# A Nystrom attention and soft-MoE kernel: batch 0 with pairs of weight blocks, a fixed order on TensorE and ScalarE, and a new schedule

## The chip, the cores and the metric

The kernel runs on one core of a Trainium2 chip. The metric is the device time of one execution in microseconds, from three runs of the kernel before the change. TensorE multiplies matrices into PSUM, ScalarE evaluates activations and copies, VectorE does element-wise work, reductions and 32 x 32 transposes, GpSimd (POOL) some element-wise work, and SyncE (SP) issues all transfers.

## The reference, cut to what matters

Three stages follow one another. Sizes: 8 batches, 8 heads, 576 positions, head size 64, 32 landmarks; d_model 512, d_ff 1536; 8 experts with 4 slots each.

```python
q_lm, k_lm = means of q and k over groups of 18 positions      # 32 landmarks
A, Bm, C = softmax(q k_lm'), softmax(q_lm k_lm'), softmax(q_lm k')
Z = Bm' / (norms); six times: Z = 2 Z - Z Bm Z                 # Newton iteration
x = A Z C v                                                     # attention, per head
x = (silu(x w_gate) * (x w_val)) w_out                          # gated layer
logits = x phi; dispatch = softmax over tokens; combine = softmax over slots
out = combine @ experts(dispatch' @ x)                          # soft mixture of experts
```

The weights w_gate, w_val and w_out come as 64-bit floats (their 32-bit values are wanted), which the kernel converts itself.

## The kernel before, in words

**Loop.** A batch has 12 units (j = 0 to 11), one for each block of 128 of the 1536 hidden columns. The product A Z C v is never formed: E holds the transposed softmax A in a high and a low part, and G, a product of the batch's small matrix WB (Z C v) with weight block j, is formed for each unit (`g_product`, line 741; ScalarE rounds it to GH at line 766, VectorE makes the rest GL at line 780). A unit (`unit`, line 949) multiplies G with E, for each half of 288 positions: six matmuls into pg (the gate), six into pv (the value), each as EH GH + EL GH + EH GL (`mm3`, line 940). ScalarE makes u = silu(pg) (line 963, issued by `in_order` at line 313), VectorE hT = u * pv (line 975). hT then gives the logits (`logits`, line 786, tile l), and VectorE transposes it into HB (`transposes`, line 798).

**Slots.** After each group of six matmuls `unit` calls `slot(i)`, so a batch has 48 slots, and slot 4j+i stands behind group i of unit j. All other work is traced in slots: the table `SCHED` gives for each piece of it the slot. `u0` says for batch 0 in which of the four slots of a unit the next G product, the logits of the unit before, and the transposes are issued; `w` and `o` give first slot and span of the conversion of each block of w_cat (gate and value) and of w_out; `p` the slot in which a converted block of w_out is transposed on TensorE (m_wt, `p_transposes`), and the distances to its product with phi (m_p) and to the last step (m_ps, into P_sb, which the logits of that unit need); `at1` and `am1` the slots of the 34 steps of batch 1's attention (`attention`, line 545) and of the 17 steps of its softmax of A (`a_softmax`, line 700); `loads` the order of the first loads in SP's queue; `lv` the slot in which v of batch 2 is loaded. Steps for slots below 0 run ahead of the loop, some of them within batch 0's own attention (`first_attention`, line 362).

**Conversions** (`conversion`, line 230). A block of w_cat (1024 words per partition) or w_out (512) takes one ScalarE instruction for the top bits (`f32_top`, line 177), then on VectorE, for each 512 words, a shift (line 193) and a scalar_tensor_tensor that ors in the low bits (line 194). With `lw` set, ScalarE makes the low bits of the whole block (line 184) and VectorE has only one scalar_tensor_tensor for each 512 words (line 190). At its end a block starts the load of the next one into the same stage (`loads_after`, line 218); w_out has two stages in turn. Converted w_out blocks are also stored to DRAM for the end of the kernel.

**Order.** A scheduler may reorder the instructions of an engine within their dependencies. `keep_order` (line 74) pins an engine to the order of the program. Before the change it pins TensorE from batch 1 on (line 1138), and nothing else. `in_order` keeps exps and silus of ScalarE in their order, since each of the two needs a table load when it follows the other. From batch 1 on, three half units near the exps use Tanh (line 960) and one more VectorE instruction (line 961) in place of Silu.

**Pairs.** `paired` (line 738) says where two units share one G product of 512 columns instead of two of 256: batches 1 to 6 before the change.

**PSUM.** g, m_a, m_c, m_t, m_v, m_wt, m_p and m_ps rotate through three banks (tag x), pg and pv through two each.

Of the kernel before, what the change touches and what calls it, by code (L numbers as in the profile page):

```python
# [10 lines left out]
AF = mybir.ActivationFunctionType  # L11
# [11 lines left out]
NJ = DFF // 128  # L23
# [2 lines left out]
SEG = S // M  # L26

SCHED = {
# [23 lines left out]
}  # L52


# [1 line left out]
def nystrom_softmoe_kernel(  # L56
# [144 lines left out]
    def load_w(j):  # L201
        g = W_STAGE[j]
        t = (big(g, f"wr{j}") if g[0] == "w" else part(int(g[0]), int(g[1]))).bitcast(U64)
        sp.dma_start(t, w_cat[j])
        raw["w", j] = t
# [84 lines left out]
    S_ = SCHED  # L290
# [40 lines left out]
    def landmark(nm, b, hp, dst):  # L331

        with tc.issue_after(fence["sum"]) if "sum" in fence else nullcontext():
            dve.tensor_reduce(dst[:, hp, :], qk_t[nm, b, hp].rearrange("p (m s) -> p m s", s=SEG),
                              axis=AX.X, op=ALU.add)
# [209 lines left out]
    def attention(b):  # L545
        assert b == 1 or ("q", b - 1) in seq
        ks, qs = landmark_tiles()
        for nm, dst in (("k", ks), ("q", qs)):
            for hp in range(4):
                (landmark_pool if b == 1 and S_["lp"][2 * hp + (nm == "q")] else landmark)(nm, b, hp, dst)  # L550
                if hp == 3 and b > 1:
                    load_four("q" if nm == "k" else "k", b)
                yield
        def score_tiles(name):
            ms = [psp.tile([128, 512], F32, tag="pv" if i == 3 else "x", name=name, bufs=2 if i == 3 else 3)
                  for i in (3, 0, 1, 2)]
            return {(1, 1): ms[0], (0, 0): ms[1], (0, 1): ms[2], (1, 0): ms[3]}
# [22 lines left out]
        for name, product, eviction in (  # L580
                ("m_a", lambda half, ms: scores(ms, ks, "q", b, half, range(4)), a_eviction),
                ("m_c", c_product, c_eviction)):
            if together:
                t = score_tiles(name)
                for half in (1, 0):
                    product(half, [t[half, 0], t[half, 1]])
                for half, r in ((1, 1), (0, 0), (0, 1), (1, 0)):
                    eviction(half, r, t[half, r])
                    yield
            else:  # L590
                for half in range(2):
                    ms = [psp.tile([128, 512], F32, tag="x", name=name, bufs=3) for r in range(2)]
                    product(half, ms)
                    for r in range(2):
                        eviction(half, r, ms[r])
                        yield
        if b == 1:
            e_tiles(b)
        elif b < nb - 1:
            load_four("k", b + 1)  # L600
# [135 lines left out]
    G_t = {}  # L736

    def paired(b, j):
        return 0 < b < nb - 1 and not (b == nb - 2 and j >= NJ - 2)

    def g_product(b, j, n):

# [206 lines left out]
    def unit(b, j, slot):  # L949
# [3 lines left out]
        for half in range(2):  # L953
            pg = psp.tile([128, 512], F32, tag="pg", name="pg", bufs=2)
            mm3(pg, b, j, 0, half)
            u = mp.tile([128, HALF], F32, tag="u", name="u", bufs=2)
            by_tanh = 0 < b < nb - 1 and (j, half) in TANH[b > 1]
            if by_tanh:

                act.activation(u, pg[:, 0:HALF], AF.Tanh, scale=0.5)  # L960
# [18 lines left out]

    WARM = [3, 4, 3, 2, 2]  # L980

    TANH = [{(3, 1), (4, 0), (4, 1)}, {(1, 1), (2, 0), (2, 1)}]
    GROUPS = [2, 2, 4, 8, 8, 8, 4]


# [30 lines left out]
                next(gens[c], None)  # L1016

    first_attention(side)
    load_w(5)
    for f in side_pre:  # L1020
        f()
# [74 lines left out]
            todo[48 * a + r].append(sm)  # L1096
    prev = None
    n_ins = lambda: len(nc.cur_bb.bb.instructions)
    for b in range(nb):
        if b == 1:  # L1100
            middle = n_ins()
        for j in range(NJ):
            p = prev
            def slot(i):
# [24 lines left out]
                if not first:  # L1129
                    for gen in todo[48 * b + n]:  # L1130
                        next(gen, None)
                if n == (46 if b == 0 else 45) and b + 1 < nb:
                    g_unit(b + 1, 0)
                if n == (47 if b == 0 else 46):
                    g_low()

            prev = (b, j, *unit(b, j, slot))
# [209 lines left out]
```

## Time and profile before

| | us |
|---|---|
| median of 3 runs | 661.8 (661.73 to 662.54) |
| the profiled execution | 661.27 |
| its span in the profile | 659.2 |
| ahead of the loop | 0 to 39.4 |
| batch 0 on TensorE | 39.4 to 124.3 |
| batches 1 to 7 | 124.3 to some 577 |
| experts and output | 577 to 659 |

The granted TensorE clock is 1.00 from 40 us of the span up to its last slice. Over the span TensorE is busy for 94%, VectorE 72%, ScalarE 46%, GpSimd 11%. Times in the rows are microseconds from the start of the span, unless a mean is given in nanoseconds. A matmul's end is modelled, so a busy TensorE may still be waiting between two matmuls: starts are what to go by.

### The profile page before, as it was taken

To read this page: it belongs to the slowest core of one execution; us is meant where nothing else is said; L and a number is where in the kernel's file an instruction comes from. 1 tells how busy PE (TensorE), PEld (TensorE's weight loads), DVE (VectorE), ACT (ScalarE), POOL (GpSimd) and SP (SyncE) were. 2 spreads that over 40 slices of the span, in tenths; PEclk is the share of its full clock that TensorE was granted. 3 is DMA by queue.
4 is the path that set the end of the run, shared out by engine and by line. 5 is a ranking of instruction groups with operands and counts; after the bars stand their busy time and mean duration, and the time that the engine had idled before them with its cause. 6 is when DMAs were issued, how large, how long until landed. Compare 5 with 4: busy or idle time off the path is not lost. (4 is left out here: it accounts for less than half of the span.)

```text
span 659.2 us, 18308 instructions
## 1 busy us (share of the span) xinstructions
PE 620.1 (94%) x7591; PEld 464.7 (70%) x7591; DVE 471.8 (72%) x1154; ACT 300.1 (46%) x764; POOL 72.6 (11%) x81
## 2 busy tenths in 40 slices
PE   5699899999999999999999999999999999989991
PEld 2576677777777877777777877787778877743561
DVE  4999989889578687859785978597857555550441
ACT  2566985465338223823382338233822442320441
POOL 0410012013011101210120013001300000010000
PEclk9699999999999999999999999999999999999996
DMA  7889774453022222222222231222130596599999
GB/s 283 280 300 340 297 269 146 123 180 95 2 74 85 76 73 77 85 75 73 91 69 75 73 108 55 73 73 74 24 122 2 146 387 223 205 327 348 348 371 330
DMA packets 63298, 106.47 MB, mean 162 GB/s; under 512 B 4976, under 2 KB 33008, under 8 KB 61680
## 3 DMA queue, kind: packets, MB, share of 16 engines
q1 hardware_dynamic: 63216, 105.32, 47.6%
q8 instruction: 59, 0.97, 0.6%
q14 instruction: 23, 0.19, 0.1%
HBM read 91.24 MB, written 12.58 MB: 158 GB/s over the span
## 5 line engine op out<-in xcount | busy, mean ns | idle before, releaser
L313 ACT ACTIVATE u<-pg 128x288 f32<-128x288 f32 x174 | 71.9, 413 | 161.3 <-PE pg L946 152.7
L975 DVE TENSOR_TENSOR hT<-u,pv 128x288 f32<-128x288 f32 x174 | 78.0, 449 | 44.2 <-PE pv L946 37.9
L946 PE MATMUL pg<-EH,GH 128*128 128x288 f32 x384 | 93.9, 325 | 2.3 <-ACT u L313 1.4
L780 DVE TENSOR_TENSOR GL<-g,GH 128x512 fp32r<-128x512 f32 (+1 forms) x122 | 65.5, 568 | 33.6 <-ACT GH L766 33.6
L946 PE MATMUL pg<-EH,GL 128*128 128x288 f32 x384 | 86.1, 299 | 1.4 <-DVE GL L780 1.0
L946 PE MATMUL pv<-EH,GH 128*128 128x288 f32 x384 | 84.3, 299 | 0.3 <-ACT GH L766 0.3
L946 PE MATMUL pg<-EL,GH 128*128 128x288 f32 x384 | 82.7, 296 | 0.0
L946 PE MATMUL pv<-EL,GH 128*128 128x288 f32 x384 | 82.3, 295 | 0.0
L946 PE MATMUL pv<-EH,GL 128*128 128x288 f32 x384 | 82.1, 294 | 0.0
L766 ACT CAST GH<-g 128x512 fp32r<-128x512 f32 (+1 forms) x122 | 54.2, 496 | 55.1 <-PE g L749 55.0
L946 PEld LDWEIGHTS pg<-EH,GH 128*128 128x128 f32 x384 | 59.6, 189 | 25.2 <-issue 18.0
L800 DVE STREAM_TRANSPOSE HB<-hT 128x576 f32<-128x576 f32 x96 | 74.3, 774 | 1.8
L946 PEld LDWEIGHTS pg<-EH,GL 128*128 128x128 f32 x384 | 62.3, 188 | 5.1 <-DVE GL L780 4.2
L946 PEld LDWEIGHTS pv<-EH,GH 128*128 128x128 f32 x384 | 61.6, 188 | 2.4 <-issue 1.8
L946 PEld LDWEIGHTS pg<-EL,GH 128*128 128x128 f32 x384 | 61.6, 188 | 0.7 <-issue 0.7
L946 PEld LDWEIGHTS pv<-EL,GH 128*128 128x128 f32 x384 | 61.5, 188 | 0.7 <-issue 0.7
L946 PEld LDWEIGHTS pv<-EH,GL 128*128 128x128 f32 x384 | 61.6, 188 | 0.5 <-issue 0.5
L749 PE MATMUL g<-w,WB 64*32 64x512 f32 (+1 forms) x976 | 56.5, 510 | 0.4 <-ACT WB L536 0.4
L795 PE MATMUL l<-hT,P_sb 128*32 128x160 f32 (+1 forms) x768 | 44.7, 298 | 1.5 <-DVE hT L975 1.1
L795 PEld LDWEIGHTS l<-hT,P_sb 128*32 128x32 f32 x768 | 15.1, 108 | 40.4 <-DVE hT L975 15.8
L914 PE MATMUL m_d<-HB,HB 32*32 32x384 f32 x864 | 35.2, 491 | 0.0
L914 PE MATMUL m_d<-HB,DN 32*32 32x384 f32 x288 | 35.1, 491 | 0.0
(248 smaller groups left out, 940.4 us busy)
## 6 DMA issues: line engine op xcount, KB each, us to landing
k<-in_kT_dram SPq DMA_DIRECT2D x52, 288.0 KB, 3.8
ffn<-in_w_dram SPq DMA_DIRECT2D x13, 1024.0 KB, 8.8
ffn<-in_w_dram SPq DMA_DIRECT2D x24, 512.0 KB, 8.8
HB<-in_w_cat_dram SPq DMA_DIRECT2D x8, 1024.0 KB, 8.4
v<-in_v_dram SPq DMA_DIRECT2D x8, 1024.0 KB, 5.9
q<-in_qT_dram SPq DMA_DIRECT2D x28, 288.0 KB, 3.0
HB<-in_w_out_dram SPq DMA_DIRECT2D x12, 512.0 KB, 6.2
wr<-in_w_cat_dram SPq DMA_DIRECT2D x4, 1024.0 KB, 9.1
```

Of the source, the lines that this page charges most:

```text
L313: i = act.activation(*a, **kw)
L749: pe.matmul(gs[r][32 * hp:32 * hp + 32, 0:256 * n].rearrange("p (u f) -> p u f", u=n), WB[b % 2][64 * r:64 * r + 64, hp, :], w[64 * r:64 * ...
L766: act.copy(H_, g)
L780: dve.tensor_tensor(out=GL, in0=g, in1=GH, op=ALU.subtract)
L795: pe.matmul(L[32 * c:32 * c + 32, 0:32 * k], P_sb[:, j, :], main[:, 0:k, c, :], start=j == 0, stop=j == NJ - 1)
L800: dve.transpose(HB[b % 2][:, S * j:S * j + S].rearrange("p (t r) -> p t r", r=32), hT[:, 0:S].rearrange("p (t r) -> p t r", r=32))
L914: pe.matmul(ms[a][32 * g:32 * g + 32, 0:384].rearrange("p (j f) -> p j f", j=NJ), d_of(a, g, k), hb[32 * a:32 * a + 32, :, 4 * k + g, :], ...
L946: pe.matmul(ps[:, 0:HALF], G_t[b, j, q, sel_][h], e[:, q, ts_], start=n == 0, stop=n == 5)
L975: dve.tensor_tensor(out=o, in0=u, in1=pv[:, 0:HALF], op=ALU.mult)
```

## The change

It sets a new schedule, extends the pairs to units 4 to 11 of batch 0, adds a Tanh set for batch 0, puts the q landmarks of batch 1 behind its first scores m_a, issues one Silu on a single element behind batch 0's attention, pins TensorE and ScalarE to the program's order in batch 0 (ScalarE only there), lets ScalarE make the low bits of w blocks 5 and 7 to 11, and moves batch 1's first G product from slot 46 to 45.

```diff
 SCHED = {
-    'w': [[-22, 2], [-12, 2], [0, 3], [1, 3], [6, 3], [10, 3], [14, 3], [18, 3], [20, 4], [28, 4], [24, 4], [33, 4]],
-    'o': [[-6, 1], [3, 2], [5, 3], [9, 3], [13, 3], [17, 3], [21, 3], [25, 3], [29, 3], [33, 3], [37, 3], [41, 3]],
-    'p': [[0, 2, 2], [5, 2, 1], [10, 2, 1], [14, 2, 1], [18, 2, 1], [22, 2, 1], [26, 2, 1], [30, 2, 1], [34, 2, 1], [38, 2, 1], [42, 2, 1], [46, 1, 0]],
-    'loads': ['w1', 'q0', 'o0', 'w0', 'v0', 'o1', 'q1', 'v1', 'w2', 'w4', 'p', 'w3'],
-    'at1': [1, 2, 3, 3, 4, 5, 6, 6, 7, 7, 8, 8, 9, 9, 10, 10, 12, 13, 13, 13, 16, 17, 18, 19, 20, 21, 22, 26, 28, 31, 34, 37, 40, 43],
-    'am1': [20, 21, 22, 22, 24, 24, 26, 27, 28, 30, 32, 34, 36, 37, 39, 41, 42],
+    'w': [[-22, 2], [-12, 2], [1, 4], [5, 4], [7, 5], [9, 4], [13, 4], [16, 4], [20, 4], [24, 4], [28, 4], [32, 4]],
+    'o': [[-6, 1], [0, 3], [2, 4], [6, 4], [10, 4], [14, 4], [18, 4], [22, 4], [26, 4], [30, 4], [34, 4], [38, 4]],
+    'p': [[-1, 2, 2], [3, 2, 2], [7, 2, 2], [11, 2, 2], [15, 2, 2], [19, 2, 2], [23, 2, 2], [27, 2, 2], [31, 2, 2], [35, 2, 2], [39, 2, 2], [43, 2, 2]],
+    'loads': ['w1', 'q0', 'o0', 'w0', 'v0', 'o1', 'q1', 'w2', 'w3', 'w4', 'p', 'v1'],
+    'at1': [0, 0, 1, 2, 3, 4, 7, 8, 8, 9, 9, 10, 11, 12, 15, 16, 16, 18, 18, 19, 20, 21, 23, 23, 23, 24, 27, 29, 31, 33, 35, 37, 39, 43],
+    'am1': [11, 12, 13, 13, 19, 19, 27, 28, 29, 30, 33, 35, 37, 38, 39, 40, 44],
...
-    'u0': [1, 3, 3, 0],
+    'u0': [1, 1, 1, 0],
...
-    'lw': [0, 0, 0, 0, 0, 0, 0, 0, 0, 0, 0, 0],
+    'lw': [0, 0, 0, 0, 0, 1, 0, 1, 1, 1, 1, 1],
...
-    'lv': 26,
+    'lv': 28,
 }
...
     def attention(b):
...
-        for nm, dst in (("k", ks), ("q", qs)):
+        def landmarks(nm, dst):
             for hp in range(4):
-                (landmark_pool if b == 1 and S_["lp"][2 * hp + (nm == "q")] else landmark)(nm, b, hp, dst)
+                landmark(nm, b, hp, dst)
                 if hp == 3 and b > 1:
                     load_four("q" if nm == "k" else "k", b)
                 yield
+
+        yield from landmarks("k", ks)
+        if b > 1:
+            yield from landmarks("q", qs)
...
+                if name == "m_a":
+                    yield from landmarks("q", qs)
...
     def paired(b, j):
-        return 0 < b < nb - 1 and not (b == nb - 2 and j >= NJ - 2)
+        return (b > 0 or j >= 4) and b < nb - 1 and not (b == nb - 2 and j >= NJ - 2)
...
-            by_tanh = 0 < b < nb - 1 and (j, half) in TANH[b > 1]
+            by_tanh = b < nb - 1 and (j, half) in TANH[min(b, 2)]
...
-    TANH = [{(3, 1), (4, 0), (4, 1)}, {(1, 1), (2, 0), (2, 1)}]
+    TANH = [{(4, 1), (5, 0), (5, 1)}, {(3, 1), (4, 0), (4, 1)}, {(1, 1), (2, 0), (2, 1)}]
...
     first_attention(side)
+    in_order("silu", warm, one, AF.Silu)
     load_w(5)
...
+    middle = n_ins()
     for b in range(nb):
         if b == 1:
-            middle = n_ins()
+            keep_order(mybir.EngineType.Activation, middle, n_ins())
...
-                if n == (46 if b == 0 else 45) and b + 1 < nb:
+                if n == 45 and b + 1 < nb:
                     g_unit(b + 1, 0)
-                if n == (47 if b == 0 else 46):
+                if n == 46:
                     g_low()
```

The line `keep_order(mybir.EngineType.PE, middle, n_ins())` behind the loop stays; with `middle` taken ahead of the loop it now covers batch 0 too.

## Rows read from the trace of the kernel before

**Rows 1.** Busy time of each engine in three stretches of batch 0 (start:end, length, engines)

```profile
39.40:72.50 33.10, 30.65 (x355) 21.39 (x356) 30.85 (x69) 24.40 (x54) 2.50 (x2) 1.00 0.89 325
72.50:108.00 35.50, 34.69 (x418) 26.19 (x414) 32.20 (x83) 27.91 (x67) 5.05 (x4) 1.00 0.73 270
108.00:124.30 16.30, 16.30 (x172) 12.41 (x171) 15.60 (x33) 7.68 (x22) 1.34 (x2) 1.00 0.51 154
```

**Rows 2.** Waits of TensorE from 39.4 to 124.3: us in total, times, longest

```profile
PE pg L946 <- ACT u L313: 1.4, 2, 0.9
PE pg L946 <- ACT GH L766: 0.9, 1, 0.9
```

**Rows 3.** TensorE in order of time, batch 0 and batch 1 (start, length, what)

```profile
107.05 0.53 PE L946 MATMUL pv<-EH,GH 128*128 128x288 f32 x2
...
108.04 0.66 PE L749 MATMUL g<-w,WB 64*32 64x256 f32 x16
108.63 0.41 PE L285 MATMUL m_ps<-cst,HB 128*128 128x32 f32 x2
...
111.52 0.47 PE L795 MATMUL l<-hT,P_sb 128*32 128x160 f32 x8
111.91 0.54 PE L946 MATMUL pg<-EH,GH 128*128 128x288 f32 x2
...
122.28 1.09 PE L749 MATMUL g<-w,WB 64*32 64x512 f32 x16
123.30 0.54 PE L946 MATMUL pv<-EH,GH 128*128 128x288 f32 x2
...
124.30 0.47 PE L795 MATMUL l<-hT,P_sb 128*32 128x160 f32 x8
124.55 0.43 PE L279 MATMUL m_p<-HB 128*32 128x128 f32 x8
...
133.83 0.53 PE L946 MATMUL pg<-EH,GH 128*128 128x288 f32 x2
...
137.20 0.47 PE L795 MATMUL l<-hT,P_sb 128*32 128x160 f32 x8
```

**Rows 4.** Groups of ScalarE's instructions, 39.4 to 124.3 (busy us, mean ns of one)

```profile
L313 ACT ACT_TABLE_LOAD x5 | 6.4, 1283 | 0.9 <-DVE stat L609 0.9
L177 ACT ACTIVATE w<-HB 128x1024 f32<-128x1024 f32 x6 | 6.9, 1155 | 0.0
L313 ACT ACTIVATE CE<-CE,stat 128x576 f32<-128x576 f32 (+1 forms) x4 | 2.2, 552 | 0.0
L313 ACT ACTIVATE AN<-AN 128x576 f32<-128x576 f32 x2 | 1.4, 684 | 0.0
```

**Rows 5.** Groups of VectorE's instructions, 39.4 to 124.3

```profile
L780 DVE TENSOR_TENSOR GL<-g,GH 128x256 fp32r<-128x256 f32 x24 | 9.1, 414 | 0.0
L193 DVE TENSOR_SCALAR w<-w 128x512 int32<-128x512 int32 x20 | 7.8, 414 | 0.6 <-ACT w L177 0.3
```

**Rows 6.** VectorE in order of time, around 102, 125 and 147

```profile
102.63 1.65 DVE L193 TENSOR_SCALAR HB<-HB 128x512 int32<-128x512 int32 x1
...
125.03 1.28 DVE L780 TENSOR_TENSOR GL<-g,GH 128x512 fp32r<-128x512 f32 x2
...
147.13 0.44 DVE L961 SCALAR_TENSOR_TENSOR u<-u,pg 128x288 f32<-128x288 f32 x1
```

**Rows 7.** ScalarE in order of time, around 70

```profile
69.63 1.28 ACT L313 ACT_TABLE_LOAD   x1
70.93 0.41 ACT L313 ACTIVATE u<-pg 128x288 f32<-128x288 f32 x1
```

**Rows 8.** Transfers of w_out blocks: count, size, median us from issue to landing

```profile
HB<-in_w_out_dram SPq DMA_DIRECT2D x12, 512.0 KB, 6.2
```

**Rows 9.** SyncE's issues in order of time: the load of v for batch 1

```profile
34.95 0.38 SPq L166 DMA_DIRECT2D v<-in_v_dram  x1
```

**Rows 10.** GpSimd in order of time, around 102

```profile
102.33 1.67 POOL L727 TENSOR_TENSOR EL<-AT,EH 128x576 fp32r<-128x576 f32 x1 [4.94 <-ACT EH L726]
```

## The prediction

> **What bounds the kernel now.** I read the profile in this order: busy time by stretch, TensorE's waits, its instructions in order of time, then the groups and timelines of ScalarE and VectorE, last the transfers. A slot is a quarter of a unit, numbered 0 to 47 in a batch; unit j covers slots 4j to 4j+3.
>
> The change touches batch 0 and what stands ahead of it. On TensorE batch 0 runs from the first G product at 39.4 to the first logits of batch 1 at 124.3, 84.9 us in three stretches (slots to 17, to 37, and the rest) [rows 1]. VectorE is busy for 30.85 + 32.20 + 15.60 = 78.65 us of them, 93%; ScalarE for 24.40 + 27.91 + 7.68 = 59.99, 71%. TensorE itself looks 96% busy, and its recorded waits are few: 1.4 us on u and 0.9 us on GH, both from ScalarE [rows 2]. The reader must not stop there: in batch 0 TensorE's busy time is padded. One group of six matmuls that is followed by another kind of work takes 0.99 us (107.05 to 108.04), while 24 in one stream take 3.37 us, 0.84 for six (133.83 to 137.20) [rows 3]. Each interruption so costs 0.15 us. I counted 42 runs of pg/pv matmuls in TensorE's timeline of batch 0, three or four per unit: logits, m_p, m_ps, m_wt and the attention pieces are scattered. So batch 0 is held by VectorE's load and by interruptions, and the later batches are out of reach of this change.
>
> **TensorE's part.** *Pinned order and new slots.* In the code as changed, slot 4j+1 carries G product, logits and m_p together, slot 4j+3 carries m_ps, m_wt and all of batch 1's attention products (3, 7, 11, 15, 23, 27, 31, 35, 39, 43; the m_n of 29, 33, 37 stand in 4j+1). That is two interruptions per unit, 24 for 42: 18 x 0.15 = -2.7 us. Logits followed by m_p take 0.25 us (124.30 to 124.55) where logits followed by pg take 0.39 (111.52 to 111.91) [rows 3]: 12 x 0.14 = -1.7 us. *Grouping.* A single G product takes 0.59 us (108.04 to 108.63), a double one 1.02 (122.28 to 123.30) [rows 3]; units 4 to 11 become four doubles: 8 x 0.59 - 4 x 1.02 = -0.6 us. With these, 5.0 us, TensorE wants 79.9 us with all its waits, and 77.6 without its 2.3 of waits [rows 2]. The other bound is a count of its pieces at undisturbed durations, which I put near 73 as an estimate: it would also mend the two G products that now alternate with other work.
>
> **ScalarE's part.** Five table loads of 1283 ns lie in the stretch [rows 4]. The new Silu on one element draws one of them to before the loop, behind the Newton iteration, where ScalarE has gaps; units (4,1), (5,0), (5,1) by Tanh, leave, as in the later batches, one load into exp and Tanh and one back to Silu: -3 x 1.28 = -3.85 us. Eight G conversions become four doubles, about -0.5 us. Six conversions of w now take their low half from ScalarE: no row shows this Copy from a quarter-stride source. Its nearest row is the Prelu of the same 1024 elements, 1155 ns [rows 4]; below I allow half of that, above twice; I take 1.1: +6.6 us (3.5 to 13.9). Sum +2.2, to about 62 us of ScalarE in 79: not the bound on average. It is uneven, though: the four exps of C (2.2 us) and the two of A (1.4) [rows 4], which stood at slots 13 and 24, now stand in slots 18 and 19 with a table load in front, and the order is pinned.
>
> **VectorE's part.** The same six conversions lose two shifts each. A shift lasts 414 ns [rows 5] and starts some 0.34 before the next instruction: 12 x 0.34 = -4.1 us. The low word is or-ed in by an instruction of the same kind and size as now. GL of two single blocks is four instructions of 414 ns [rows 5], of a double block two in 1.28 us [rows 6]: about -0.1 per block, -0.5 in all with their overlap. Three Tanh halves each add a scalar_tensor_tensor of 0.44, some 0.37 as it overlaps [rows 6]: +1.1 us. The four q landmarks move behind m_a (slots 8 to 10) and the softmax of A to slots 27 to 44: moved work, the same count, and VectorE has no idle place that would hide it, so it costs nothing only as long as nobody waits for it. Demand: 78.65 - 4.1 - 0.5 + 1.1 = 75.1 us.
>
> **A rule on table loads.** Behind the load at 69.63, which lasts 1.28, the next u starts at 70.93, 0.02 later [rows 7]; so I price a load at 1.28. The Trainium skill (ScalarE: Activation LUTs, What ACT_TABLE_LOAD costs) counts a drain of about 1.38 us on top of each switch, 2.66 in all; the trace shows no such time behind this one. By the page the three loads would give back 8.0 us of ScalarE, an estimate.
>
> **Transfers.** The landing of a w_out block is 6.2 us [rows 8]. From block 2 on, a conversion now begins at slot 4j-6, and the stage it uses is loaded again when it ends, two slots later, for the block eight slots on: six slots or 9.6 us, for an issue of 0.4 and 6.2. Covered by 3 us as long as VectorE's last step is on time. In the queue of SP the load of v for batch 1, which can only go out at 34.95 [rows 9], no longer stands ahead of w2, w3, w4 and phi; these go out while it still waits, and v and w5 follow. v is wanted at slot 27. The stores and reloads of w_out move a slot or three earlier with their conversions and pass no other waiting transfer. Worth: w2 and w3 are there when the loop starts; VectorE, which then had q landmarks to fill with, gains nothing that it isn't charged for above. Ahead of the loop the first m_wt can run before the first G product instead of after it, and the table load leaves the first u's path: 0 to -0.6, I take -0.3.
>
> **The sum.** TensorE wants 73 to 79.9 us, VectorE 75.1. Before, VectorE was busy 93, 91 and 96% in the three stretches [rows 1]; with TensorE as close behind it, I take 95%: 75.1 / 0.95 = 79.1 us for 84.9, -5.8. With -0.3 ahead of the loop it is -6.1. The profiled execution took 661.27 us (span 659.2), 0.5 below the median of 661.8; so 655.2 there, and 655.8 against the median: 656.0, rounded. The share at 91% gives 82.5 (-2.4), at 98% 76.6 (-8.3): 653.5 to 659.5 for this case alone.
>
> **Rivals.** *TensorE's floor* (12%): VectorE's queue fits between, waits go to the level of later batches. 73 + 1.5 = 74.5 us, -10: 651.5. For it: the even spread of the new slots. Against: VectorE at 100%.
>
> *The heap in slots 18 and 19* (22%): table load, six exps, two halves of Tanh, m_wt's and m_p's copies in one fixed queue: 1.3 + 3.6 us ahead of everything else in 3 us of TensorE's time. GH of units 6 and 7 (slot 21), the copies of m_wt and m_p and the u of slot 20 all stand behind it, and the pinned TensorE waits at m_ps. Priced at 3 us on top of the forecast: 659. For it: both waits of TensorE [rows 2] are this very thing, in two smaller doses.
>
> *Vector work arriving late behind a pinned queue* (slower, 12%): the top half of each w_out conversion is an instruction of ScalarE in fixed order; if it waits for its transfer, u and GH wait behind it. It decides once VectorE ends a conversion more than the 3 us of cover late. Then ten blocks each wait about 1 us, of which TensorE, also pinned, pays nearly all, and the forecast's 6 us become +3: 664.8. For it: 93% busy, and a shift that stood beside GpSimd's 1.67 us product [rows 10] took 1.65 us instead of 0.41 [rows 6]; the Trainium skill (GPSIMD Engine Reference, Key points) says that the two share SBUF interfaces, and the trace agrees. Four such products of A are moved into slots 29, 30, 39 and 40, beside conversions of w and w_out: 4 x 1.2 = 5 us at worst for 2 to 3 now. Against: the conversions lose 4.1 us of VectorE.
>
> *It does little* (8%): the program's order may already be what ran, so that pinning changes nothing; then pairing gives 0.6 and the loads are off the path: 661.2. Against it: the scattered order [rows 3].
>
> **How the numbers follow.** The forecast has 46%, the rivals 12, 22, 12 and 8. Faster by over 0.2% (1.3 us, about what a measurement of this kernel tells from no change): 46 + 12 + 21 = 79%; within 0.2%: 9%; slower: 12%. The range 650.5 to 662.5 leaves out the slower case and a little below the floor.
>
> **What would show it.** Right: VectorE over 94% busy in the first 70 us after the first G product, TensorE's timeline with two interruptions per unit, two table loads in batch 0, the first G product of batch 1 near 115 (122.28 less the gain and one slot). Wrong: waits of TensorE on u or GH above 3 us together (the heap); ScalarE waiting on w_out transfers (the slower case); VectorE under 88% with TensorE still waiting, which would mean that order, not load, sets the time.

## The result, and the profile after

The change makes the kernel slower: 666.21 us (median of 6 runs, 664.48 to 667.90) for 661.90 (6 runs on the same chip), a ratio of 1.0063 with a 95% interval of 1.0047 to 1.0079. The forecast was 656.0. The profiled execution after took 664.48 us, the shortest of the six, and its span is 662.7; before, 661.27 and 659.2. What follows explains the 3.5 us between these two executions, not the whole 4.3 between the medians.

First, where the 3.5 us between the two spans lie. The busy time by stretch, cut at the first G product of batch 0, the first of batch 1, the last of batch 7 and the end (start:end, length; PE, PEld, DVE, ACT, POOL busy; granted TensorE clock; DMA share; GB/s), for the kernel before:

```profile
0.00:39.44 39.44, 24.82 (x244) 16.61 (x244) 29.23 (x69) 16.05 (x39) 9.18 (x14) 0.87 0.76 261
39.44:122.28 82.84, 79.62 (x912) 58.97 (x912) 76.59 (x180) 58.48 (x139) 8.89 (x7) 1.00 0.77 274
122.28:569.15 446.87, 444.03 (x5646) 348.78 (x5645) 334.49 (x821) 199.13 (x524) 49.81 (x49) 1.00 0.30 99
569.15:659.20 90.05, 71.63 (x792) 40.34 (x791) 31.48 (x86) 26.40 (x63) 4.70 (x11) 0.94 0.99 327
```

and for the kernel after:

```profile
0.00:39.86 39.86, 24.85 (x248) 16.79 (x249) 28.49 (x67) 16.82 (x40) 9.62 (x14) 0.91 0.92 330
39.86:123.48 83.62, 76.59 (x855) 59.90 (x854) 74.72 (x168) 60.27 (x135) 9.62 (x7) 0.96 0.70 239
123.48:569.06 445.58, 443.49 (x5639) 349.02 (x5635) 332.03 (x818) 198.57 (x523) 49.85 (x49) 1.00 0.30 98
569.06:662.70 93.64, 71.96 (x792) 40.31 (x791) 31.57 (x86) 26.38 (x63) 4.76 (x11) 0.94 0.96 315
```

The lengths differ by +0.4, +0.8, -1.3 and +3.6 us. Batch 0, which the change rewrites, is 0.8 longer where 5.8 less were forecast, although TensorE and VectorE both have less to do in it (76.59 for 79.62, 74.72 for 76.59), and its granted clock is no longer 1.00. The largest loss lies in the last 94 us, whose code the change doesn't touch. Of the 1.3 us gained in batches 1 to 7, 0.9 lie in batch 1, which takes 67.5 for 68.4 from its first G product to that of batch 2.

Inside batch 0 the starts of G products, before and then after, cut out unit 1 and units 6 and 7:

```profile
42.42 0.66 PE L749 MATMUL g<-w,WB 64*32 64x256 f32 x16
49.30 0.66 PE L749 MATMUL g<-w,WB 64*32 64x256 f32 x16
...
78.91 0.66 PE L749 MATMUL g<-w,WB 64*32 64x256 f32 x16
94.45 0.62 PE L749 MATMUL g<-w,WB 64*32 64x256 f32 x2
```

```profile
42.98 0.66 PE L755 MATMUL g<-w,WB 64*32 64x256 f32 x16
52.86 1.11 PE L755 MATMUL g<-w,WB 64*32 64x256 f32 x16
...
98.49 1.09 PE L755 MATMUL g<-w,WB 64*32 64x512 f32 x16
```

A unit is counted here from its G product to the next unit's. Unit 1 takes 9.9 us for 6.9. Units 6 and 7, which share the G product at 78.58 (shown below), take 19.9 for 15.5. The other nine units together take 53.8 for 60.4. So a gain of 6.6 us, more than the 5.8 forecast, did come, in part because work was moved out of these units; two places lost 7.4.

**Batch 0.** TensorE's waits from 39.86 on, to be held against [rows 2] (total, times, longest):

```profile
PE m_a L542 <- ACT P_sb L286: 2.1, 1, 2.1
PE m_ps L285 <- ACT HB L280: 1.7, 1, 1.7
PE m_t L638 <- ACT P_sb L286: 1.6, 1, 1.6
```

All three end at copies on ScalarE. What held the first is in ScalarE's order of time:

```profile
45.46 0.43 ACT L313 ACTIVATE u<-pg 128x288 f32<-128x288 f32 x1
48.60 0.66 ACT L177 ACTIVATE HB<-HB 128x512 f32<-128x512 f32 x1 [2.70 <-DMA HB<-in_w_out_dram]
49.16 0.17 ACT L286 COPY P_sb<-m_ps 128x32 f32<-128x32 f32 x1
49.23 0.59 ACT L271 COPY HB<-m_wt 128x512 f32<-128x512 f32 x1
```

and in TensorE's:

```profile
46.57 0.67 PE L542 MATMUL m_a<-q,ks 64*32 64x288 f32 x2
49.38 0.44 PE L542 MATMUL m_a<-q,ks 64*32 64x288 f32 x3 [2.14 <-ACT P_sb L286]
...
51.29 0.68 PE L952 MATMUL pv<-EH,GH 128*128 128x288 f32 x2
51.77 0.68 PE L952 MATMUL pv<-EL,GH 128*128 128x288 f32 x2
```

The top half of w_out block 2, pinned in ScalarE's queue, waits 2.70 us for its transfer. The copies of m_ps and m_wt stand behind it, the PSUM bank that m_a wants is not free, and TensorE, pinned too, stands for 2.14 us. From about 50.5 pairs of matmuls start 0.48 apart, where 0.27 is the step elsewhere: the granted clock falls to the lower level, 0.50 of full speed (1.2 of 2.4 GHz). The same happens after the stalls in units 6 and 7. Both stretches (the columns as above):

```profile
50.50:53.90 3.40, 3.40 (x28) 2.31 (x26) 1.18 (x3) 0.41 (x1) 0.00 (x0) 0.50 0.94 348
88.00:91.40 3.40, 3.40 (x16) 3.33 (x16) 3.40 (x13) 3.26 (x8) 0.00 (x0) 0.50 0.67 195
```

In both TensorE is busy for all 3.40 us, so busy time doesn't show the loss. In the first it is 1.7 us, half the stretch: unit 1 takes 9.9 us, and 6.0 in a version with neither stall nor half clock there (e2_wout_later below, G products at 45.30 and 51.33); the 3.9 between them are the 2.1 of wait and 1.7. For the second no such price is shown; pairs of executions of the same code (below, at h1_three_again) speak against it.

The transfer is late because of what lies ahead of it in SyncE's queue and on the DMA engines. The queue's issues after, the counterpart of [rows 9]:

```profile
35.24 0.38 SPq L166 DMA_DIRECT2D v<-in_v_dram  x1
35.66 0.52 SPq L167 DMA_DIRECT2D v<-in_v_dram  x1
39.53 0.35 SPq L204 DMA_DIRECT2D wr<-in_w_cat_dram  x1
39.93 0.43 SPq L248 DMA_DIRECT2D wo_dram<-HB  x1
40.40 0.43 SPq L215 DMA_DIRECT2D HB<-in_w_out_dram  x1
```

The block goes out at 40.40, behind v and w_cat block 5. That load (39.53) had held the queue, since it waited for TensorE's m_w, and over the whole flight of the w_out block the DMA engines are full (the last but one column):

```profile
SPq L204 <- PE m_w L535: 3.2, 1, 3.2
```

```profile
40.40:48.60 8.20, 6.24 (x64) 4.46 (x56) 8.00 (x17) 3.94 (x11) 0.00 (x0) 1.00 1.01 326
```

It is used 8.20 us later (48.60), where [rows 8] have 6.2 as the median, and ScalarE stood ready from 45.90, 5.5 us behind the issue.

In units 6 and 7 ScalarE runs from 73.3 to 93 us without a gap. A cut of that run, with the counterpart of TensorE behind it:

```profile
82.30 0.40 ACT L966 ACTIVATE u<-pg 128x288 f32<-128x288 f32 x1
82.59 1.12 ACT L177 ACTIVATE w<-HB 128x1024 f32<-128x1024 f32 x1
83.62 1.06 ACT L772 CAST GH<-g 128x512 fp32r<-128x512 f32 x2
84.56 0.29 ACT L280 COPY HB<-m_p 128x128 f32<-128x128 f32 x1
84.72 1.19 ACT L184 ACTIVATE HB<-HB 128x1024 int32<-128x1024 uint16 x1
```

```profile
78.58 2.26 PE L755 MATMUL g<-w,WB 64*32 64x512 f32 x16
...
84.90 0.41 PE L285 MATMUL m_ps<-cst,HB 128*128 128x32 f32 x2 [1.67 <-ACT HB L280]
...
87.83 0.99 PE L638 MATMUL m_t<-cst,CE 128*128 128x128 f32 x4 [1.61 <-ACT P_sb L286]
```

The copy that m_ps needs (84.56) stands behind a table load, the exps, w8's top and GH. The double G product at 78.58 takes 2.26 where the others take 1.09: it has a stall of 1.2 us inside, which is in no list of waits.

**The tail.** Inside the m_d products of the last batch TensorE pauses and waits for nothing that the profile shows:

```profile
584.61 0.48 PE L920 MATMUL m_d<-HB,DN 32*32 32x384 f32 x1
586.44 0.83 PE L920 MATMUL m_d<-HB,HB 32*32 32x384 f32 x4 [1.35 <-issue]
```

In the third part of the page of the profile a queue of its own carries instructions. Its size fits TensorE's code: 59 packets of 16 KB for 2 x 7527 matmuls and weight loads make 64 bytes for one instruction, 256 for a packet. In the trace a packet of it runs from 584.05 to 585.12, just ahead of the pause; before, packets run at 574.54 and 586.41, on either side of m_d. The pairs of batch 0 take 128 instructions from TensorE (7591 to 7527 of each kind), half a packet. The four weight loads of the experts that m_d's end releases go out from 587.32 on, not 585.27, and the transfers, the bound of the tail, lose a stretch. The same window before and then after:

```profile
585.00:590.00 5.00, 4.26 (x33) 2.14 (x30) 3.97 (x13) 0.32 (x1) 2.98 (x4) 1.00 0.98 318
```

```profile
585.00:590.00 5.00, 3.60 (x27) 1.76 (x22) 2.60 (x6) 0.09 (x1) 2.87 (x4) 1.00 0.60 191
```

### The profile page after: what moved, and what is told of

It is laid out like the page before. It is cut to its first block, busy times and chain, and to the rows that moved or that the text cites. A ratio compares the mean times of both kernels' runs of the same rounds, so it can differ in the third digit from the quotient of the medians.

```text
span 662.7 us, 18185 instructions
## 1 busy us (share of the span) xinstructions
PE 616.9 (93%) x7527; PEld 466.0 (70%) x7527; DVE 466.8 (70%) x1137; ACT 302.0 (46%) x761; POOL 73.8 (11%) x81
## 5 line engine op out<-in xcount | busy, mean ns | idle before, releaser
L981 DVE TENSOR_TENSOR hT<-u,pv 128x288 f32<-128x288 f32 x171 | 76.6, 448 | 44.6 <-PE pv L952 40.3
L952 PE MATMUL pv<-EH,GH 128*128 128x288 f32 x384 | 82.6, 296 | 0.0
L801 PEld LDWEIGHTS l<-hT,P_sb 128*32 128x32 f32 x768 | 15.1, 108 | 44.0 <-DVE hT L981 15.8
```

The lines of the kernel that those rows point to most:

```text
L801: pe.matmul(L[32 * c:32 * c + 32, 0:32 * k], P_sb[:, j, :], main[:, 0:k, c, :], start=j == 0, stop=j == NJ - 1)
L952: pe.matmul(ps[:, 0:HALF], G_t[b, j, q, sel_][h], e[:, q, ts_], start=n == 0, stop=n == 5)
L981: dve.tensor_tensor(out=o, in0=u, in1=pv[:, 0:HALF], op=ALU.mult)
```

## The experiments

Seventeen runs were made, each in five rounds beside the kernel before, on five chips (one for each group of names, e1 to e4, e5 to e8, f, g and h); sixteen kernels, one of them twice (f3 and h1). Median and ratio are over the executions of a run. The rest of the ledger comes from TensorE's instructions in one profiled execution, which lies up to 2.6 us off its median; f3 and h1 agree within 0.3 us in each of the four lengths. The columns: start (to the first G product), batch 0 (to the first of batch 1), batches 1 to 7 (to the last G product), tail (to the end of the span), and where in the tail instruction packets start, counted from that last G product. The first m_d product starts at 10.6 there in all of them; the last column has the start of the last one.

| kernel | median | ratio, 95% | start | batch 0 | 1 to 7 | tail | packets at | last m_d |
|---|---|---|---|---|---|---|---|---|
| before | 661.9 | | 39.4 | 82.8 | 446.9 | 90.0 | 5.4, 17.3 | 15.6 |
| after | 666.2 | 1.0047-1.0079 | 39.9 | 83.6 | 445.6 | 93.6 | 15.0, 18.4 | 17.7 |
| e1_no_pairs | 662.1 | 0.9991-1.0018 | 40.5 | 83.8 | 446.5 | 90.3 | 1.7, 16.8 | 15.6 |
| e2_wout_later | 660.7 | 0.9975-1.0002 | 42.2 | 78.7 | 445.8 | 93.8 | 15.1, 18.7 | 17.9 |
| e3_scalar_free | 661.3 | 0.9969-1.0003 | 41.4 | 81.0 | 446.0 | 91.2 | 15.0 | 15.6 |
| e4_no_low_by_scalar | 663.6 | 1.0014-1.0053 | 41.8 | 80.7 | 447.2 | 94.3 | 15.6, 18.9 | 18.2 |
| e5_later_b6 | 661.8 | 0.9983-1.0013 | 39.5 | 79.5 | 451.3 | 90.9 | 1.7, 16.8 | 15.6 |
| e6_before_b6 | 666.3 | 1.0055-1.0085 | 38.3 | 82.9 | 452.1 | 92.0 | 15.4 | 15.6 |
| e7_after_b6 | 665.3 | 1.0035-1.0066 | 39.7 | 85.7 | 448.9 | 90.8 | 1.6, 17.4 | 15.6 |
| e8_later_b6_low78 | 661.5 | 0.9984-1.0023 | 40.8 | 81.2 | 448.6 | 91.1 | 1.7, 16.9 | 15.6 |
| f1_no_silu | 665.6 | 1.0031-1.0074 | 38.4 | 85.3 | 446.0 | 94.3 | 15.5, 19.0 | 18.3 |
| f2_later_no_pairs | 659.5 | 0.9953-0.9981 | 40.9 | 81.0 | 446.7 | 90.9 | 5.8, 16.6 | 15.6 |
| f3_later_no_pairs_no_silu | 658.8 | 0.9939-0.9965 | 39.1 | 81.1 | 445.9 | 90.9 | 5.5, 17.3 | 15.6 |
| f4_f3_scalar_free | 661.8 | 0.9984-1.0002 | 39.3 | 83.7 | 446.2 | 91.1 | 5.9, 16.9 | 15.6 |
| g1_w_later | 661.3 | 0.9984-1.0011 | 39.9 | 84.8 | 446.3 | 91.2 | 6.1, 17.0 | 15.6 |
| g2_ct_spread | 660.8 | 0.9976-1.0001 | 39.8 | 81.1 | 446.5 | 90.8 | 5.8, 17.5 | 15.6 |
| g3_both | 661.2 | 0.9985-1.0007 | 39.1 | 83.2 | 446.2 | 91.2 | 5.4, 16.9 | 15.6 |
| h1_three_again | 658.9 | 0.9955-0.9979 | 39.0 | 80.8 | 446.0 | 90.9 | 5.9, 16.7 | 15.6 |
| h2_only_o2_later | 658.9 | 0.9956-0.9979 | 39.1 | 80.3 | 445.8 | 90.0 | 3.7, 17.1 | 15.6 |

### The tail: pairs and TensorE's code

```diff
-        return (b > 0 or j >= 4) and b < nb - 1 and ...
+        return 0 < b < nb - 1
```

> The changed kernel with batch 0's G products unpaired again, so that TensorE has its 128 instructions back. Theory (the end of the kernel lost 3.5 us because the fetch of TensorE's next block of code fell into the dense m_d products of the last batch's tail): the pause of 1.8 us inside m_d near 584.6 goes, the span from the last batch's last G product (569.1) to the end goes from 93.6 back to about 90.1 us, batch 0 pays 0.6 to 1.2 us for the unpaired products, and the time is about 662 to 663 where the changed kernel shows 664.5. Rival (the loss at the end comes from something else, such as the order of loads or the run itself): the tail keeps its 93.6 us and the time is 665 to 666.

Measured: 4.1 us less than the change by the medians. The pause is gone, the last m_d product starts at 15.6, the tail is 90.3, and batch 0 is only 0.2 longer. Giving back the instructions far from batch 0 separates the code from what batch 0 does:

```diff
-        return ... and not (b == nb - 2 and j >= NJ - 2)
+        return ... and not (b == nb - 2 and j >= NJ - 10)
```

> The changed kernel with the G products of units 2 to 9 of batch 6 taken apart and nothing else. Theory of the code blocks: no pause in m_d, tail 90 us instead of 93.6, unpaired products 0.6 to 1.0 us, so 663.5 against the changed kernel's median of 666.2; batch 0 as in the changed kernel, with both stalls. Rival: the tail keeps 93.6 us and the time is 666 to 667.

> The kernel before, with the G products of units 2 to 9 of batch 6 taken apart and nothing else: 128 instructions more on TensorE, which by blocks of 256 puts the edge where 128 fewer put it. Theory of the code blocks: a pause of 1 to 2 us inside m_d appears, the tail from the last G product to the end goes from 90.0 to about 93.5 us, the unpaired products cost 0.6 to 1.0, and the time is 665 to 666 where the kernel before takes 661.8. Rival: no pause, 662.5.

Measured: the edit is the same, and it moves the tail in opposite ways. In the changed kernel the pause goes and the tail falls from 93.6 to 90.8; in the kernel before, a pause appears and it grows from 90.0 to 92.0. There the packet starts at 15.4 and the pause lies just behind m_d, in the matmuls on the tile warm. TensorE's waits in the tail of e6_before_b6:

```profile
PE warm L808 <- issue: 1.6, 1, 1.6
```

The mechanism held; two sizes did not. The pause in the kernel before is a wait of 1.6 us, and its tail grows by 2.0, not 3.5. And taking 8 units of batch 6 apart costs 3.3 us, not 0.6 to 1.0: batch 6 takes 67.1 for 63.8 in e5, e7 and e8, by the starts of its first G products. In e6 it takes 68.6, and 3.4 us of that batch ran at half clock. Batch 0 of e7 is also 2.1 longer than that of the changed kernel, with the same code. So the whole time hides what the tail gained: only the ledger tells the two theories apart.

In all rows of the ledger a packet that starts between 15.0 and 15.6 goes with a pause of 1.0 us or more, and where none starts there, there is no such pause. Four of the six pauses lie inside m_d (the changed kernel, e2, e4, f1), with tails of 93.6 to 94.3 us. Two lie behind it, with less or no loss: 92.0 in e6, and in e3 91.2, where the kernels without a pause have 90.0 to 91.2. How the packet stops the engine isn't shown.

### The first stall: w_out's transfer

```diff
-    'o': [[-6, 1], [0, 3], [2, 4], [6, 4], [10, 4], ... [38, 4]],
+    'o': [[-6, 1], [0, 3], [4, 3], [8, 3], [12, 3], ... [40, 3]],
```

> The changed kernel with the w_out conversions of blocks 2 to 11 begun two slots later (one slot ahead of where they began in the kernel before), all else as changed. Theory (a conversion of w_out on the pinned ScalarE waits 2.7 us for its transfer, the copies of the first scores stand behind it, TensorE stands for 2.1 us and then goes 3.4 us at half clock): ScalarE's wait for that transfer at 46 to 48.6 goes, TensorE's wait at m_a and the stretch of half clock near 50.5 to 53.9 go, the first scaled product of batch 1 comes about 3.5 to 4 us sooner, and the time is about 661. Rival (the copies wait for their place in ScalarE's queue anyway, or the time comes back as a wait at a later slot): less than 1 us.

Measured: 5.5 us less by the medians. ScalarE's wait and TensorE's wait at m_a are gone, batch 0 is 4.9 shorter, and up to 55 us its clock stays up:

```profile
39.00:55.00 16.00, 14.76 (x167) 10.97 (x166) 14.89 (x32) 9.39 (x23) 0.00 (x0) 1.00 0.86 298
```

The 3.9 of unit 1 are most of the 4.9. The tail keeps its pause (93.8), as the code theory wants.

With batch 6 taken apart on top of it (the edit of e7_after_b6):

```diff
-        return ... and not (b == nb - 2 and j >= NJ - 2)
+        return ... and not (b == nb - 2 and j >= NJ - 10)
```

> The kernel with the later w_out conversions (660.7 us), and the G products of units 2 to 9 of batch 6 taken apart, which gives TensorE back the 64 weight loads and 64 products that pairing takes away in batch 0, but far from batch 0. Theory (TensorE's code comes in blocks of 256 instructions, and 128 instructions fewer put a block's edge into the dense m_d products of the tail, under a full DMA load): the pause of 1.5 us inside m_d goes, the tail from the last G product to the end goes from 93.8 to about 90.2 us, the unpaired products cost 0.6 to 1.0, and the time is about 658. Rival (the tail's loss has to do with what batch 0 does): the pause stays, and the time is 661 to 662.

Measured: 661.8, a miss in the sum and a hit in its part. The tail is 2.9 shorter, batch 6 takes 3.3 more, and batch 1, which the edit doesn't touch, 2.2 more (69.8 for 67.6): 3.4 us of it, from 144.9, ran at half clock.

### The start: one table load

```diff
-    in_order("silu", warm, one, AF.Silu)
```

> The changed kernel without the one line that loads ScalarE's Silu table ahead of the loop. Theory (that load moves a conversion and the copies of the Newton steps, TensorE's products before the loop come in another order, and TensorE stands for 1.3 to 1.9 us before it at 32 us, after which some executions have a stretch of half clock): that wait is 0.4 us as in the kernel before, the first scaled product starts at 38.5 to 39.5, a table load of 1.3 us falls into the first units instead; time 0.5 to 1.5 us less than the changed kernel's 666.2, so about 665. Rival (the load ahead of the loop costs nothing, and inside the loop it would): 1.3 us more, 667.5.

In the changed kernel the load stands at 25.23, ahead of a conversion of w and of the copies of the Newton steps, and TensorE's instructions of the start come in another order: all of m_v first, then a wait for a copy behind two conversions on VectorE.

```profile
30.32 0.90 PE L419 MATMUL m_v<-v,CT 128*32 128x64 f32 x40
32.77 0.68 PE L469 MATMUL m_n<-newton 128*128 128x128 f32 x4 [1.55 <-DVE newton L503]
```

Without that line, in f1_no_silu:

```profile
29.97 0.65 PE L419 MATMUL m_v<-v,CT 128*32 128x64 f32 x32
31.02 0.49 PE L469 MATMUL m_n<-newton 128*128 128x128 f32 x2 [0.40 <-DVE newton L503]
```

The start is 1.5 shorter (38.4), as expected, and nearly all of it is lost at once: the same w_out block goes out 1.5 sooner (38.89), but is there only 0.5 sooner (48.14). ScalarE now waits 3.8 us for it, TensorE 3.4 at m_a, and batch 0 is 1.7 longer. The time is 0.6 less. Of the nine profiled executions of kernels with this load, five (e2, e3, e4, e8, f2) show a granted clock under 1.00 between 30 and 40 us, and their starts end at 40.8 to 42.2; the other four end at 39.5 to 40.5. Of the ten without it none does, and they end at 38.3 to 39.9. That the changed kernel's other runs, up to 3.4 us above its profiled one, are executions of the first sort fits this but isn't shown.

### ScalarE's pin and its low halves

```diff
-        if b == 1:
-            keep_order(mybir.EngineType.Activation, middle, n_ins())
```

> The changed kernel with ScalarE's order in batch 0 left to the scheduler, TensorE still pinned. Theory (the pin on ScalarE makes both stalls): ScalarE takes the copies of the scores ahead of the late conversion, both stretches of half clock go, and the time is 657 to 660. Rival (the stalls come from where the work was put, not from the pin): ScalarE's order hardly differs, and the time stays at 664 to 666; a third way is that the scheduler puts conversions ahead of what TensorE waits for, and the time is over 667.

```diff
-    'lw': [0, 0, 0, 0, 0, 1, 0, 1, 1, 1, 1, 1],
+    'lw': [0, 0, 0, 0, 0, 0, 0, 0, 0, 0, 0, 0],
```

> The changed kernel with all low parts of the weights converted by VectorE, none by ScalarE (6 instructions of 1.1 to 1.2 us less on ScalarE, about 4.1 us more on VectorE). Theory (ScalarE's heap of work at 73 to 93 us makes the second stall: two low parts, a table load, exponentials and a high part in one run): the heap gets 2.3 us shorter, the second stall of 4.8 us and perhaps its stretch of half clock shrink, and the time is 1 to 3 us less than the changed kernel's. Rival (VectorE is the bound of batch 0, as the prediction had it): batch 0 gets about 4 us longer and the time is 668 or more.

Measured: 4.9 and 2.7 us less by the medians, the first short of its expectation (661.3 for 657 to 660). Without the pin the copies pass the late conversion and m_a no longer waits, but one stretch of half clock stays (3.4 us from 54.2). From the G product of unit 6 to that of unit 8 it takes 15.9 us (79.76 to 95.62), like the kernel before (78.9 to 94.5, 15.6), where the changed kernel takes 19.9. So the pin is part of both stalls; its removal is no gain by itself, though: f4_f3_scalar_free (below) loses by it. Without ScalarE's low halves the second stretch of half clock is gone (1.00 from 73 to 108 us), units 6 and 7 take 16.9, and VectorE's 4.4 us more (80.05 busy for 75.61, from 39 to 125) didn't make batch 0 longer: 80.7. VectorE's load did not set the time.

### Repairs together

The edits of e1 and e2; those and f1's; and those and e3's:

> The changed kernel with w_out conversions two slots later and batch 0's G products unpaired: both repairs found so far together. Theory (they act in different places, transfers in batch 0 and code blocks in the tail): no pause in m_d, tail about 90.2 to 91 us, no stretch of half clock near 50 us, and the time is 660.7 less 3 plus 0.2 to 1, about 658.3. Rival (unpaired products cost in batch 0 what they cost in batch 6, 3.4 to 5 us for 8 units): 661 to 662.

> As the kernel with later w_out conversions and unpaired products, and also without the Silu load ahead of the loop. Theory (three separate losses): the first scaled product starts near 39 in place of 40 to 42, and the time is 1 us less, about 657.5, faster than both kernels. Rival (the table load inside the loop costs what the start gains): the same time.

> As the kernel with all three repairs, and ScalarE's order in batch 0 left to the scheduler. Theory (the pin holds copies that TensorE waits for behind conversions): the wait at m_ps and m_t near 78 to 90 us gets shorter by 1 to 2 us, time about 656.5. Rival (ScalarE is full there whatever the order): 657.5 or more.

Measured: 659.5, 658.8 and 661.8. Later w_out conversions and no pairs take 6.7 us off the changed kernel, leaving out the table load another 0.8; with all three the kernel beats both, though each of the three times lies above its expectation. Freeing ScalarE on top costs 3.0: TensorE then waits 2.3 for bd and 2.6 for low halves. The third kernel run again, the same code on another chip:

> The kernel with all three repairs once more, the same code. If its ratio of 0.9952 was that of the kernel, it comes out at 0.994 to 0.997; if it was that of few runs, at 0.998 to 1.0.

Measured: 658.9, ratio 0.9967 (0.9955 to 0.9979), inside the first expectation: this version beats both kernels.

The two executions of this code also bear on the price of the half clock in units 6 and 7. One stretch in f3 and then in h1:

```profile
80.10:86.90 6.80, 6.59 (x28) 6.00 (x28) 5.93 (x19) 6.48 (x16) 1.71 (x2) 0.50 0.81 266
```

```profile
80.10:86.90 6.80, 5.84 (x66) 4.75 (x67) 5.91 (x19) 6.71 (x16) 1.96 (x2) 1.00 0.83 266
```

Units 6 and 7 take 19.6 us in f3 (74.64 to 94.28), with 6.8 at half clock and 2.2 of recorded waits, and 19.5 in h1 (74.37 to 93.83), at full clock with 4.4 of waits. So here the slower clock cost 0.2 and for the rest took the place of waiting; ScalarE is busy for 6.48 and 6.71 of the 6.80. In e2 and e5, with the same code in batch 0, these units take 19.5 at full clock and 20.4 with 6.8 at half: 0.8. Half of the 6.8 would be 3.4.

### The second stall

```diff
-    'lw': [0, 0, 0, 0, 0, 1, 0, 1, 1, 1, 1, 1],
+    'lw': [0, 0, 0, 0, 0, 1, 0, 0, 0, 1, 1, 1],
```

> As the kernel with later w_out conversions and batch 6 taken apart, and the low parts of w7 and w8 given back to VectorE: 2.3 us less in ScalarE's run of work between the Tanh slots and the exponentials (73 to 93 us), 1.4 us more on VectorE. Theory (ScalarE's heap there makes TensorE's second stall of 4.8 us): TensorE's waits at g, m_ps and m_t near 78 to 88 us get 2 us shorter, no stretch of half clock there, and the time is about 2 us under that of the kernel without this edit, 656. Rival (VectorE is what batch 0 waits for): same time or up to 1.4 us more.

Measured on e5_later_b6 with this edit: the rival. Time 0.3 less, batch 0 1.7 longer. The wait moves from ScalarE to VectorE:

```profile
PE m_wt L270 <- DVE HB L194: 3.2, 3, 1.1
```

Then the conversions of blocks 8 to 11 were moved, or the steps of the softmax around m_t, on f3's kernel:

```diff
-    'w': [..., [20, 4], [24, 4], [28, 4], [32, 4]],
+    'w': [..., [23, 4], [27, 4], [31, 4], [35, 4]],
-    'at1': [..., 20, 21, 23, 23, 23, 24, 27, 29, ...],
+    'at1': [..., 20, 21, 24, 25, 25, 26, 27, 29, ...],
```

> The kernel with all three repairs (658.75 us), and the conversions of w8 to w11 begun three slots later (23, 27, 31, 35). Theory (the second stall is ScalarE's and VectorE's bunched work in units 6 and 7, conversions included): units 6 and 7, 19.7 us from the sixth to the eighth unit's G product, get 2 us shorter, and the time is about 657. Rival (the softmax steps alone set the length of these units): unchanged, or later units get what these lose.

> The kernel with all three repairs, and the transposes of the first scores with their copies at slots 24, 25, 25 in place of three at slot 23. Theory (bunched softmax steps make the wait at m_ps and m_t): the wait of 2.2 us at m_ps gets 1 us or more shorter, time about 657.5. Rival: the m_ps wait stays and the Newton steps of batch 1 start later, 658.8 to 659.5.

> Both of these edits together. If both causes are real and separate, they add: 656 or less. If the engines are simply full there, no more than the better of the two alone.

Measured: 661.3, 660.8 and 661.2 (0.9985 to 1.0007). None gained. In the first and third, block 10 is converted after the transposes of hT have overwritten part of its stage, so these two kernels give other numbers; their instructions and sizes are the same. g1's units 6 and 7 take 24.0 us (75.3 to 99.3), the wait is VectorE's again (3.4 at m_wt), and the expected 2 us are a miss.

```diff
-    'o': [[-6, 1], [0, 3], [2, 4], [6, 4], ...
+    'o': [[-6, 1], [0, 3], [4, 2], [6, 4], ...
```

> As the kernel with all three repairs, but only the w_out conversion of block 2 is later than in the change (slots 4 and 5); all others keep the three slots of lead. Theory (block 2's transfer was the only late one, and the lead relieves VectorE later on): no wait for the transfer, no half clock near 50 us, TensorE's waits for VectorE's low halves at m_wt go (1.9 us), and the time is 1 to 2 us under the other. Rival (block 3's or 4's transfer is then the late one, or the lead does nothing): the same time or 1 to 3 us more, with a wait of ScalarE for a w_out transfer.

Measured: 658.9, the same as with all blocks later. VectorE's low halves are in time, but TensorE waits at m_wt for a GL (1.3), at m_ps (1.7) and m_t (1.6) instead. ScalarE still waits 1.2 us for block 2, without a wait of TensorE at m_a. So block 2 alone was the transfer that cost time; the shorter lead of the others costs nothing, and the longer one gives nothing that lasts. Units 6 and 7 take 19.8 us in it, 19.5 to 20.9 in the other kernels with the pin apart from e4 and g1, and 15.9 and 16.0 without it (e3, f4); f4 then loses in unit 8, which takes 10.0 us (94.0 to 104.0) for 6.9 in f3. What of the second stall belongs to the exps and copies that the change moved there, and what to conversions, isn't settled: the softmax back in its old slots wasn't tried.

## Why the prediction was wrong

**Work on the engines: right.** VectorE's demand was put at 75.1 us; from 39.86 to 125.70 it was busy for 75.16. A double G product takes 1.02 from its start to that of the logits, and m_p follows these by 0.25, both as in [rows 3]; there are two interruptions per unit (24 runs of pg and pv matmuls from 39.86 to 125.70). The Copy that makes a low half had no row; it takes 1.16 to 1.18 us, for 1.1 taken. Two table loads of 1283 ns lie in batch 0, as forecast [rows 4]. The drain that the Trainium skill (ScalarE: Activation LUTs, What ACT_TABLE_LOAD costs) counts on top of a load doesn't show here either: the load starts at 25.23, where the copy before it ends, and the next instruction starts at 26.52.

**"I take 95%": the step of the sum that failed.** VectorE ran at 89% (74.72 of 83.62), because it had to wait for a TensorE that stood: 6.7 us of recorded waits (the three shown make 5.4), 1.2 inside a G product and 1.7 of half clock behind the first stall are 9.6. Without them batch 0 would take 74.0 from G to G, an estimate; the shortest of any run is 78.7 (e2). VectorE was not the bound: e4 gave it 4.4 us more, and batch 0 was shorter.

**"Covered by 3 us": failed first.** The cover was counted for the steady state: 9.6 us for an issue of 0.4 and a median landing of 6.2. Block 2 is the first of the new rhythm. Its load went out at 40.40, behind v, whose new place the same paragraph had described, and w5; it took 8.2 us, and its conversion was due after 5.5. That is 2.7 us of wait on ScalarE; two slots of delay for this one block are the repair. The slower rival named this very chain (a pinned top half waits for its transfer, u and copies wait behind it, TensorE pays), but laid it to VectorE's lateness in ten blocks and gave it 12%.

**The heap: right in place, too small in price.** The rival said m_ps would wait behind GH and the exps in slots 18 to 21; it does. Three us were put on it; waits at g, m_ps and m_t make 1.2 + 1.7 + 1.6 = 4.5, and units 6 and 7 are 4.4 longer than before. The half clock adds 1.7 behind the first stall, which neither price had; what it adds here isn't shown, and 6.8 us of it added 0.2 and 0.8 in the two pairs above. It doesn't fall after each stall: e2_wout_later has 2.2 and 1.0 in units 6 and 7 at full clock.

**"Where ScalarE has gaps": failed.** The load ahead of the loop reordered the start, +0.4 in the profiled execution for the -0.3 taken, and 1.4 to 2.7 in the five executions where the clock fell too.

**"The later batches are out of reach": failed, and by the most.** Batch 0's pairs were priced by their matmul time alone. The 128 instructions that they save shift TensorE's code fetches, and one falls into the densest stretch of instructions, under a full DMA load: +3.6 in the tail. That no step had: a change of the instruction count reaches everything behind it. The gain of 1.3 in batches 1 to 7 wasn't forecast either; it varies between the versions and its cause is open.

Of the signs named, ScalarE's wait on a w_out transfer came. So did the one of order instead of load: VectorE was busy for 87.6% of the forecast's stretch (75.16 of 85.84), under the 88 that were set, while TensorE waited; in the first 70 us it was 90.7%, not over 94. The heap's sign, TensorE's waits on u or GH above 3 us, did not come (0.5 on GH): its waits were for the copies of m_p and m_ps behind them. The first G product of batch 1 came at 123.48, not near 115.

## What to carry to other kernels

Count the cover of a pinned wait at its first instance, with the bytes that stand ahead of it there, not in the steady state: with the DMA engines full, an issue 1.5 us sooner brought the block 0.5 sooner. Whoever pins two engines lets one late transfer stop both. Cut the span at marks that both kernels have before explaining a difference: here the stretch that was rewritten held 0.8 of the 3.5 us, and inside it a gain of 6.6 hid behind two losses of 7.4. And when a kernel gets longer or shorter far from the edit, compare the times of the instruction fetches.

## What the hardware showed that was not expected

A fetch of 16 KB of instructions takes about 1 us at most places, yet TensorE stands 1.0 to 1.9 us when one starts in the last part of m_d (143 matmuls and 137 weight loads from 580 to 585 us in the changed kernel, the DMA engines 99% busy); from 30 us on, no other wait of TensorE of over 0.3 us in these traces is put down to "issue". A stall of 2.1 us was followed by 3.4 us at half the granted clock, which nearly doubled its price without a row of its own; in units 6 and 7, where TensorE waits in any case, 6.8 us at half clock cost 0.2 and 0.8. And repairs don't add by themselves: 1.5 us won at the start were lost again at a transfer that arrived almost when it did before.
